# Deferring two of seven pair products, plain products in the experts, and block sums moved between VectorE and GpSimd

## The chip, the cores and the metric

One core of a Trainium2 chip runs the kernel. The metric is the device time of one execution in microseconds; the times are medians of several executions.

## The reference

Three layers follow one another: causal attention with a cumulative bias (2 batches, 8 heads, 576 rows, 64 columns), a mixture of 8 experts with a relu, weighted by gates P that come out of 8 rounds of row and column normalising, and one wide layer with a softplus.

```python
def _moe_ref(x, w_gate, w1, w2):
    ...
    for e in range(E):                    # E = 8, w1[e] 512 x 1024, w2[e] 1024 x 512
        h = np.maximum(x @ w1[e], 0.0)    # x: 1152 x 512
        ye = h @ w2[e]
        out += P[:, e:e + 1] * ye

def _moe2_ref(x, w_in, w_out):            # w_in 512 x 2048, w_out 2048 x 512
    h = x @ w_in
    g = np.maximum(h, 0.0) + np.log1p(np.exp(-np.abs(h)))
    return (g @ w_out).astype(np.float32)
```

## The kernel before

All matrix products keep float32 accuracy by splitting each operand into a high part (a copy rounded by ScalarE) and a low part (the word less its high part), and adding three products: high x high, high x low, low x high.

Both dense layers are cut into blocks of 512 hidden columns, x = 0 to 19: NX = 16 blocks of the experts and 4 of the wide layer (NH = 20). The 1152 rows are two batches g = 0, 1 of 576. Work runs as a pipeline of phases. The first phase of block x (here: its A phase) makes the up products of x for batch 1 and beside them the down products of x for batch 0; the second (B) makes the up products of x + 1 for batch 0 and the down products of x for batch 1. One tile of 128 rows, number 4 (NB), lies across both batches.

The up products are made by `Unit`, a seven-product scheme: p1 to p7 for each of two units a and b, 6 matmuls of 288 columns each. Unit results leave PSUM as words of h; `evict` (L452) does that, and `defer(k, ...)` puts it off by k + 1 calls of `flush`, of which each product and each down step makes one.

The down products exist in two forms. The plain one, `downs` (L555), takes a tile of 128 rows in 4 steps of three 512-column matmuls, and `total` adds the sum to acc. The other one, `pairs` (L389), makes a batch's 512 rows with seven products of blocks, each for r = 0 and 1: 14 steps of 6 matmuls with 256 columns. Its operands are four blocks a11, a12, a21, a22 of the words, and sums s1 to s4 of them, against the four blocks b of w2 and four sums t1 to t4. The products share PSUM halves: s2, a22, s1 and s4 accumulate one behind the other on the same half, and `add_to` (L376) adds the half to acc on VectorE after each of them, so that the next one on it must wait for that add. The blocks that use `pairs` are listed in SEVEN (L130): 14, 17, 18 and 19.

The preparation: `h_steps` (L322) makes sums (L334, GpSimd), high parts (L327, ScalarE) and low parts (L330, VectorE) of a batch's blocks, with m the part of the words that belongs to tile 4. `prep_t` (L248) makes the sums t (L256, GpSimd) and `t_part` their high (L243, ScalarE) and low parts (L245, VectorE); `prep_b` (L220) the parts of the blocks b (L226 ScalarE, L228 VectorE). `sums1`, `sums2` (GpSimd) and `split` (ScalarE, VectorE) prepare w1. One work tile xw holds s3, s2, t2 and t4 in turn; `hold` guards whose it is. In prep_t of a block that follows a block with pairs, two sums are written in place over raw b11 and b12.

The order is written out by hand in strings that `play` (L1289) reads: a1 to b7 are products, d is the next step of down work, and other tokens append a generator to one of three lists (back, side, bot). After each product and each d, `step` takes one step of the first generator of each list. Every engine runs its own instructions in this program order. In the A phase before, pair steps come in twos behind a product:

```python
A7_SEQ = "E0 a1 b1 a2 b2 =0 d d a6 d d b6 d d F0 a7 d d b7 =1 d d a5 d b5 d d a3 d b3 e1 a4 d b4"
B7_SEQ = ("E1 a1 b1 =2 a2 b2 d d d d a6 d d {11} b6 d d {3} F1 a7 d b7 d {2} a5 d b5 d {4} d a3 d {1} d b3 e0 d {22} a4 d b4 d {21}")
```

The last block has no products left in its second phase; that phase is called the tail.

Of the kernel before, what the change touches and what calls it, by code (L numbers as in the profile page):

```python
# [14 lines left out]
ALU = mybir.AluOpType  # L15
# [5 lines left out]
def attention_moe_ffn(ctx, tc, q, k, v, s, w_gate, w1, w2, w_in, w_out, out):  # L21
    nc = tc.nc
    P = 128
    B, S, H, D = v.shape
# [28 lines left out]
    def f(ap):  # L53
        return ap.bitcast(F32)
# [72 lines left out]
    w2_p = []  # L127
    w2_t = []
    sp_t = {}
    SEVEN = (NX - 2, NX + 1, NX + 2, NX + 3)  # L130

    def load(x, which, i):
        if x >= NH:
# [74 lines left out]
    def seven(x):  # L208
        return x in SEVEN

# [9 lines left out]
    def prep_b(x, n):  # L220

        if x >= NH:
            return
        raw = blocks(x)[n]
        hi, lo = (w2_block(n, z) for z in w2_t)
        nc.scalar.activation(out=hi, in_=raw, func=AF.Copy)  # L226
        yield
        nc.vector.tensor_tensor(out=lo, in0=raw, in1=f(hi), op=ALU.subtract)  # L228
        if n == "21":
            load(x + 1, 2, 1)  # L230
        ready.add((x, "b" + n))
        yield
# [3 lines left out]
    def hold(who, after):  # L236
        assert held[0] in after, (held, who)
        held[0] = who

    def t_part(x, n, src, part):  # L240
        h, l = (sp_t[z][:, n - 1] for z in ("th", "tl"))
        if part == "h":
            nc.scalar.activation(out=h, in_=src, func=AF.Copy)  # L243
        else:
            nc.vector.tensor_tensor(out=l, in0=src, in1=f(h), op=ALU.subtract)  # L245
            ready.add((x, f"t{n}"))

    def prep_t(x, n, kept=True):  # L248
# [73 lines left out]
    def h_steps(x, g, part):  # L322

        z = h_sets(g)

        def high(n):
            nc.scalar.activation(out=z[n][0], in_=z[n][2], func=AF.Copy)  # L327

        def low(n):
            nc.vector.tensor_tensor(out=z[n][1], in0=z[n][2], in1=f(z[n][0]), op=ALU.subtract)  # L330
            ready.add((x, g, n))

        def sum_(o, a, b, op):
            nc.gpsimd.tensor_tensor(out=z[o][2], in0=z[a][2], in1=z[b][2], op=op)  # L334

        if part == "e":
            hold((x, g), (None,))
            sum_("s3", "a11", "a21", ALU.subtract)
            high("a11")
            yield  # L340
            low("a11")
            yield
            last = (x - 1 + g, 1 - g)
            assert not seven(last[0]) or (*last, "done") in ready
            high("s3")
            yield
        elif part == "E":
            high("m")
            high("a22")
            yield  # L350
            low("s3")
            low("m")
            low("a22")
            sum_("s2", "a22", "s3", ALU.subtract)
            yield
            sum_("s1", "a21", "a22", ALU.add)
            yield
            high("a12")
            yield
            low("a12")  # L360
            high("s2")
            yield
            sum_("s4", "a12", "s2", ALU.subtract)
            high("s1")
            yield
            low("s2")
            low("s1")
            hold(None, ((x, g),))
            yield
        else:  # L370
            high("s4")
            yield
            low("s4")
            yield

    def add_to(x, t, cols, py, first, tile_col):  # L376
        a = acc[0][:, t, cols]
# [8 lines left out]
        if x == NH - 1 and (not first or (tile_col == (0, 1))):  # L386
            nc.sync.dma_start(out=out[t * P:(t + 1) * P, cols], in_=a)

    def pairs(x, g, middle=None):  # L389

        z = h_sets(g)
        py = []
        for r in range(2):
            nd[0] += 1
            py.append(ps.tile([P, DM], F32, tag=f"y{1 + nd[0] % 2}", name="py", bufs=1))
        d = (slice(0, HW), slice(HW, 2 * HW))

        def left(k, n, c, r):
            return z[n][k][:, c, r, :]

        def right(k, n, c):
            if n[0] == "t":
                return sp_t[("th", "tl")[k]][:, int(n[1]) - 1, c, :]
            return w2_block(n[1:], w2_t[k])[:, c, :]

        for a, b, bank, start, tile_, col, first in (
# [4 lines left out]
            if a == "s3" and middle is not None:  # L411
                yield from middle
            for r in range(2):
                assert (x, g, a) in ready and ((x, b) in ready or {(x, "w", 2 * (b[1] == "2") + c) for c in range(2)} <= ready), (x, g, a, b)
                o = py[r][:, d[bank]]
                for c in range(2):
                    ops = [(left(0, a, c, r), right(0, b, c)), (left(0, a, c, r), right(1, b, c)),
                           (left(1, a, c, r), right(0, b, c))]
                    for n, (u, v) in enumerate(ops):
                        nc.tensor.matmul(o, u, v, start=(start and c == 0 and n == 0), stop=(c == 1 and n == 2),  # L420
                                         skip_group_check=True)
                flush()
                if a == "s4" and r:
                    ready.add((x, g, "done"))
                add_to(x, rows_of(g) // P + 2 * r + tile_, d[col], o, first, (tile_, col))
                yield

# [58 lines left out]
    class Unit:  # L486
# [32 lines left out]
        def p2(self):  # L519
            b = self.bank("tr")  # L520
            self.product(b, A12, B21, True)
            flush()
            nc.vector.tensor_tensor(out=b, in0=b, in1=self.v1, op=ALU.add)  # L523
            evict(self.x, 5 if seven(self.x) else 0, b, self.p, self.h0)

        def p6(self):
            self.product(self.a, S2, T2, False)
# [8 lines left out]
        def p5(self):  # L536
            self.product(self.a, S1, T1, False)
            flush()
            u4 = self.copy("v")
            t = m_t[0].tile([P, HB], F32, tag="t2", name="t2", bufs=2)  # L540
            defer(0, lambda: nc.vector.tensor_tensor(out=t, in0=self.c, in1=u4, op=ALU.add))  # L541
            evict(self.x, 1, t, self.p + 2, self.h1)

        def p3(self):
            self.product(self.a, S4, B22, False)
# [57 lines left out]
    with tc.manual_schedule():  # L603
# [680 lines left out]
        def products(x, g):  # L1284

            u = dict(a=Unit(x, 0, g), b=Unit(x, 1, g))
            return {z: getattr(u[z[0]], "p" + z[1]) for z in ORDER.split()}

        def play(seq, todo, d=None):  # L1289


            for z in seq.split():
# [11 lines left out]
                if z[0] in "xy":  # L1304
                    bot.append(prep_b(x + 1, z[1:]) if z[0] == "x" else prep_t(x + 1, int(z[1]), seven(x)))
                    continue
                if z[0] in "eEF":
                    g = int(z[1])
                    if seven(x if g else x + (z[0] == "e")):
                        side.append(h_steps(x if g else x + (z[0] == "e"), g, z[0]))  # L1310
                    continue
                if z == "n":
                    flush()
# [7 lines left out]
        B_SEQ = ("d d =2 a1 d d b1 d a2 d b2 d a6 d b6 d a7 d b7 d a5 d b5 d d w0 a3 d d w2 b3 d d w1 a4 d d w3 b4")  # L1321
        A_TURN = "a1 b1 a2 b2 d d d d a6 =0 d b6 d a7 d b7 d =1 a5 d b5 d a3 d b3 d a4 d b4 d d d"
        TURN = ("t0 d d d d u0 d d d d d a1 d b1 d a2 d =2 b2 t1 d a6 d b6 d a7 d b7 d a5 d b5 d d u1 w0 a3 w2 b3 w1 a4 w3 b4")
        A7_SEQ = "E0 a1 b1 a2 b2 =0 d d a6 d b6 d d F0 a7 d d b7 =1 d d a5 d b5 d d a3 d b3 e1 a4 d b4"
        A7_LAST = "E0 a1 b1 a2 b2 d a6 d d b6 d d F0 a7 d d b7 d d a5 d b5 d a3 d b3 e1 a4 b4 d d"
        B7_SEQ = ("E1 a1 b1 =2 a2 b2 d d d d a6 d d {11} b6 d d {3} F1 a7 d b7 d {2} a5 d b5 d {4} d a3 d {1} d b3 e0 d {22} a4 d b4 d {21}")
        TO_SEVEN = B_SEQ.replace("b2", "b2 y3 y2 y4 y1").replace("b3", "b3 e0")
        B7 = {True: {"11": "x11 x12 y0", "3": "y3", "2": "y2", "4": "y4", "1": "y1", "22": "x22", "21": "x21"},
              False: {"11": "w0 w1", "3": "", "2": "", "4": "", "1": "", "22": "", "21": "w2 w3"}}
        A_GROUPS = [(0, 1), (2,), (3,)]  # L1330
        B_GROUPS = [(4,), (5,), (6,), (7, 8)]

        def then(*parts):
            for z in parts:
                yield from z
# [6 lines left out]
        for x in range(NH):  # L1342
# [6 lines left out]
            if x == NX - 2:  # L1349
                nc.scalar.preload_act_table_set("softplus")  # L1350
            if seven(x):
                play(A7_SEQ if x + 1 < NH else A7_LAST, products(x, 1), pairs(x, 0))
            else:
                play(A_SEQ if x != NX else A_TURN, products(x, 1), downs(x, A_GROUPS))
            if x == NX:
# [5 lines left out]
                own = open_blocks()  # L1361
            if seven(x):
                if x + 1 < NH:
                    seq = B7_SEQ
                    for k, z in B7[seven(x + 1)].items():
                        seq = seq.replace("{" + k + "}", z)
                    play(seq, products(x + 1, 0), then(downs(x, [(NB,)]), pairs(x, 1)))
                else:
                    play("E1 n n n n " + "d " * 8 + "F1 " + "d " * 10, {}, pairs(x, 1, downs(x, [(NB,)], "tr")))
                if not seven(x + 1):  # L1370
                    rest()
                    own.close()
                continue
# [70 lines left out]
```

## Time and profile before

| what | us |
|---|---|
| median of 3 runs | 1088.13 (1088.04 to 1088.27) |
| profiled execution | 1089.59 |
| its span, first to last instruction | 1087.80 |
| TensorE busy | 1056.2 |
| VectorE busy | 799.5 |
| ScalarE busy | 525.3 |
| GpSimd busy | 406.1 |

The profile shows one execution. Busy time of TensorE is that of matmuls in flight, which overlap, so its share is near 100% whenever it has work; starts of consecutive matmuls give the real pace. In rows of single instructions the columns are start, duration, engine, line and names, and in brackets the idle time in front and what ended it.

### The profile page before, as it was taken

How to read it: one execution, taken by the hardware profiler on the slowest of the kernel's cores; microseconds unless marked ns; L12 is line 12 of the kernel's file. 1: busy time of each engine (PE TensorE's matmuls, PEld its weight loads, DVE VectorE, ACT ScalarE, POOL GpSimd, SP SyncE). 2: the span in 40 equal slices, each digit the busy share in tenths (PEclk: the TensorE clock that was granted, in tenths of full speed). 3: DMA queues.
4: the chain of work that ended last, by engine and by line, in shares of the span. 5: the costliest groups of instructions: out<-in, count | busy, mean ns of one | idle time of the engine just before them, and what ended most of it. 6: DMA issues, size and time to landing. Idle time of an engine off the chain costs nothing.

```text
span 1087.8 us, 18435 instructions
## 1 busy us (share of the span) xinstructions
PE 1056.2 (97%) x6876; PEld 942.5 (87%) x6876; DVE 799.5 (73%) x1725; ACT 525.3 (48%) x1232; POOL 406.1 (37%) x449
## 2 busy tenths in 40 slices
PE   6999999999999999999999999999999999999987
PEld 4777888889888888988888898888899888898987
DVE  5576566667877878787887888775477487678876
ACT  6998544334443433434343343334454365555542
POOL 8885303053342414134241423423262233546321
PEclk9999999999999999999999999999999999999999
DMA  6221111122232222223222231311111011201002
GB/s 195 78 83 55 39 40 39 40 92 96 89 130 88 80 97 98 100 77 124 91 74 98 97 107 68 127 59 39 39 40 59 20 40 39 78 21 59 1 16 73
DMA packets 31538, 78.47 MB, mean 72 GB/s; under 512 B 5856, under 2 KB 13024, under 8 KB 31448
## 3 DMA queue, kind: packets, MB, share of 16 engines
q1 hardware_dynamic: 28704, 68.69, 18.9%
q0 software_dynamic: 2560, 8.39, 2.0%
q8 instruction: 54, 0.88, 0.3%
q14 instruction: 36, 0.29, 0.1%
q10 hardware_dynamic: 184, 0.20, 0.1%
HBM read 65.99 MB, written 10.75 MB: 71 GB/s over the span
## 4 chain that ended last, share of the span: by engine, by line
PE 82%; DVE 10%; ACT 3%; issue 2%; POOL 2%; DMA 0%; POOLq 0%; ACTq 0%; DVEq 0%
PE py L578 36%; PE ph L502 35%; PE py L420 5%; DVE hl L330 2%; PE sc L794 2%; POOL eb L857 1%; PE pv L901 1%; DVE sl L330 1%; PE tr L875 1%; DVE xl L1198 1%; DVE acc L381 1%; DVE xt L1229 1%; DVE ph L523 1%; PE sc L798 1%; DVE w1l L155 1%
## 5 line engine op out<-in xcount | busy, mean ns | idle before, releaser
L502 PE MATMUL ph<-xh,w1h 128*128 128x288 f32 x1120 | 331.7, 296 | 0.3 <-ACT v L510 0.3
L502 PE MATMUL ph<-xh,w1l 128*128 128x288 f32 x1120 | 330.8, 295 | 0.0
L502 PE MATMUL ph<-xl,w1h 128*128 128x288 f32 x1120 | 329.3, 294 | 0.0
L578 PE MATMUL py<-w2h,hh 128*128 128x512 f32 x588 | 233.5, 397 | 1.0 <-DVE acc L590 1.0
L578 PE MATMUL py<-w2l,hh 128*128 128x512 f32 x588 | 232.5, 395 | 0.2 <-POOL w2l L201 0.2
L578 PE MATMUL py<-w2h,hl 128*128 128x512 f32 x588 | 232.4, 395 | 0.0
L502 PEld LDWEIGHTS ph<-xh,w1h 128*128 128x128 f32 x1120 | 210.0, 188 | 18.4 <-ACT v L510 0.5
L502 PEld LDWEIGHTS ph<-xl,w1h 128*128 128x128 f32 x1120 | 210.4, 188 | 16.9
L502 PEld LDWEIGHTS ph<-xh,w1l 128*128 128x128 f32 x1120 | 210.3, 188 | 0.0
L510 ACT ACTIVATE v<-ph 128x288 f32<-128x288 f32 x160 | 64.0, 409 | 187.5 <-PE ph L502 184.8
L469 ACT ACTIVATE hh<-ph 128x288 fp32r<-128x288 f32 x180 | 73.7, 411 | 151.8 <-DVE ph L552 78.2
L578 PEld LDWEIGHTS py<-w2h,hl 128*128 128x128 f32 x588 | 110.5, 188 | 26.5
L201 POOL TENSOR_TENSOR w2l<-raw,w2h 128x512 fp32r<-128x512 f32 x36 | 51.3, 1427 | 215.9 <-ACT w2h L199 215.9
L596 DVE SCALAR_TENSOR_TENSOR acc<-py,gate,acc 128x512 f32<-128x512 f32 x118 | 88.0, 746 | 49.2 <-PE py L578 49.0
L1166 POOL TENSOR_TENSOR cm<-cm,ct 128x512 f32<-128x512 f32 x32 | 45.1, 1408 | 201.5 <-DVE ct L1164 201.5
L578 PEld LDWEIGHTS py<-w2h,hh 128*128 128x128 f32 x588 | 110.4, 188 | 10.5 <-DVE acc L590 1.2
L578 PEld LDWEIGHTS py<-w2l,hh 128*128 128x128 f32 x588 | 110.5, 188 | 10.0 <-POOL w2l L201 0.7
L155 DVE TENSOR_TENSOR w1l<-raw,w1h 128x512 fp32r<-128x512 f32 (+1 forms) x160 | 109.8, 686 | 11.3 <-ACT w1h L152 11.3
L476 DVE SCALAR_TENSOR_TENSOR hl<-ph,hh 128x288 fp32r<-128x288 f32 x180 | 81.2, 453 | 26.7 <-ACT hh L469 25.1
L152 ACT ACTIVATE w1h<-raw 128x512 fp32r<-128x512 f32 (+1 forms) x160 | 91.1, 571 | 0.0
L541 DVE TENSOR_TENSOR t<-ph,v 128x288 f32<-128x288 f32 x80 | 36.4, 455 | 54.5 <-ACT v L510 53.9
L510 ACT ACTIVATE u<-ph 128x288 f32<-128x288 f32 x80 | 32.7, 411 | 55.5 <-PE ph L502 53.4
(246 smaller groups left out, 1779.2 us busy)
## 6 DMA issues: line engine op xcount, KB each, us to landing
raw<-in_w SPq DMA_DIRECT2D x64, 512.0 KB
f<-in_w_in SPq DMA_DIRECT2D x16, 512.0 KB
f<-in_w_out SPq DMA_DIRECT2D x16, 512.0 KB
wd<-cm POOLq DMA_DIRECT2D x32, 256.0 KB, 3.1
raw<-wd SPq DMA_DIRECT2D x16, 512.0 KB
vv<-in_v SPq DMA_DIRECT2D x8, 256.0 KB
out<-acc SPq DMA_DIRECT2D x16, 128.0 KB
qk<-in_k SPq DMA_DIRECT2D x7, 288.0 KB
```

Source lines behind the costliest of these rows:

```text
L152: nc.scalar.activation(out=hi[:, o], in_=t[:, src], func=AF.Copy)
L155: nc.vector.tensor_tensor(out=lo[:, o], in0=t[:, src], in1=f(hi[:, o]), op=ALU.subtract)
L201: (nc.gpsimd if i else nc.vector).tensor_tensor(out=lo, in0=t[:, r], in1=f(hi), op=ALU.subtract)
L420: nc.tensor.matmul(o, u, v, start=(start and c == 0 and n == 0), stop=(c == 1 and n == 2), skip_group_check=True)
L469: nc.scalar.activation(out=hh, in_=z, func=AF.Relu)
L476: nc.vector.scalar_tensor_tensor(out=hl, in0=z, scalar=0.0, in1=f(hh), op0=ALU.max, op1=ALU.subtract)
L502: nc.tensor.matmul(o, u, v, start=(start and c == 0 and n == 0), stop=(c == 1 and n == 2), skip_group_check=True)
L510: nc.scalar.activation(out=t, in_=self.a, func=AF.Copy)
L541: defer(0, lambda: nc.vector.tensor_tensor(out=t, in0=self.c, in1=u4, op=ALU.add))
L578: nc.tensor.matmul(py[t], u, v, start=(k == 0 and n == 0), stop=(k == NF - 1 and n == 2))
L596: nc.vector.scalar_tensor_tensor(out=a, in0=py, scalar=gate_t[0][:, t, e:e + 1], in1=a, op0=ALU.mult, op1=ALU.add)
L1166: nc.gpsimd.tensor_tensor(out=m, in0=m, in1=f(t), op=ALU.add)
```

## The change

SEVEN loses block 14, so that no block of the experts uses pair products. In h_steps the sums go from GpSimd to VectorE; in prep_b and t_part the low parts go from VectorE to GpSimd. The last two of the seven pair products (s4 and a12, four steps) of a batch are made in the phase behind, in front of its own down work, one behind each of the first four products; each of the other ten pair steps then stands behind one product. The steps of h_steps begin with their phase (part E, 13 steps; F is s4's high and low part) instead of in the phase before (part e). The words of p2 and p5 are deferred further. The parts of b22 and b21 are made in the A phase (X22, X21) instead of at the end of the B phase before.

```diff
-    SEVEN = (NX - 2, NX + 1, NX + 2, NX + 3)
+    SEVEN = (NX + 1, NX + 2, NX + 3)
...   prep_b, t_part
-        nc.vector.tensor_tensor(out=lo, in0=raw, in1=f(hi), op=ALU.subtract)
+        nc.gpsimd.tensor_tensor(out=lo, in0=raw, in1=f(hi), op=ALU.subtract)
...
-            nc.vector.tensor_tensor(out=l, in0=src, in1=f(h), op=ALU.subtract)
+            nc.gpsimd.tensor_tensor(out=l, in0=src, in1=f(h), op=ALU.subtract)
...   h_steps
-            nc.gpsimd.tensor_tensor(out=z[o][2], in0=z[a][2], in1=z[b][2], op=op)
...
+            nc.vector.tensor_tensor(out=z[o][2], in0=z[a][2], in1=z[b][2], op=op)
+        if part == "F":
+            assert (x, g, "s3 done") in ready
             high("s4")
             yield
             low("s4")
             yield
+            return
+        hold((x, g), (None,))
+        sum_("s3", "a11", "a21", ALU.subtract)
+        high("m")
+        yield
+        high("a11")
+        low("m")
+        yield
+        high("a22")
+        low("a11")
+        yield
+        low("a22")
+        yield
+        last = (x - 1 + g, 1 - g)
+        assert not seven(last[0]) or (*last, "s4 done") in ready
+        high("s3")
+        yield
+        low("s3")
+        yield
+        sum_("s2", "a22", "s3", ALU.subtract)
+        yield
+        high("a12")
+        yield
+        sum_("s1", "a21", "a22", ALU.add)
+        yield
+        high("s2")
+        yield
+        low("s2")
+        yield
+        low("a12")
+        high("s1")
+        yield
+        sum_("s4", "a12", "s2", ALU.subtract)
+        low("s1")
+        hold(None, ((x, g),))
+        yield
...   Unit.p2, Unit.p5
-            evict(self.x, 5 if seven(self.x) else 0, b, self.p, self.h0)
+            evict(self.x, 8 if seven(self.x) else 0, b, self.p, self.h0)
...
-            evict(self.x, 1, t, self.p + 2, self.h1)
+            evict(self.x, 4 if seven(self.x) else 1, t, self.p + 2, self.h1)
...   the order
+        A7_SEQ = ("E0 a1 ~ b1 ~ {22} a2 ~ b2 ~ {21} =0 a6 d b6 d a7 d b7 d F0 =1 a5 d b5 d a3 d b3 d a4 d b4 d")
+        B7_SEQ = ("E1 a1 d b1 d a2 d b2 d =2 a6 d d b6 d d {12} a7 d d {11} b7 d d {3} F1 a5 d b5 d {2} a3 d b3 d {4} a4 d b4 d {1}")
+        B7 = {True: {"12": "x12", "11": "x11 y0", "3": "y3", "2": "y2", "4": "y4", "1": "y1"},
...
+        A7 = {True: {"~": "d", "{22}": "X22", "{21}": "X21"}, False: {"~": "", "{22}": "", "{21}": ""}}
+        LAST = "E1 d d D d D d D D d d d d F1 " + "d " * 10
...
+                d = then(d if seven(x - 1) else (), pairs(x, 0))
+                play(seq, products(x, 1), d)
...
+                    d = then(d, downs(x, [(NB,)]), pairs(x, 1))
...
+                    play(LAST, {"D": lambda: next(middle)}, then(d, pairs(x, 1)))
```

## Rows read from the trace of the kernel before

**Rows 1.** The page's first part: busy time and share by engine.
```profile
PE 1056.2 (97%) x6876; PEld 942.5 (87%) x6876; DVE 799.5 (73%) x1725; ACT 525.3 (48%) x1232; POOL 406.1 (37%) x449
```

**Rows 2.** Windows: blocks 13, 14, 17, 18, block 19's first phase, tail.
```profile
core 0: us, PE busy (x) PEld busy (x) DVE busy (x) ACT busy (x) POOL busy (x), PEclk, DMA share, GB/s
742.77:790.25 47.48, 47.48 (x279) 42.56 (x277) 25.05 (x47) 18.84 (x45) 15.26 (x15) 1.00 0.13 45
790.25:839.85 49.60, 45.85 (x352) 44.70 (x351) 39.68 (x75) 25.63 (x57) 18.60 (x16) 1.00 0.16 54
942.30:993.03 50.73, 46.34 (x350) 44.61 (x349) 42.09 (x72) 27.93 (x62) 25.83 (x21) 1.00 0.12 42
993.03:1043.29 50.26, 46.31 (x350) 44.59 (x349) 42.15 (x74) 27.20 (x61) 24.40 (x20) 1.00 0.07 22
1043.29:1066.32 23.03, 21.52 (x170) 21.11 (x168) 16.03 (x32) 10.51 (x25) 5.53 (x4) 1.00 0.10 35
1066.32:1087.80 21.48, 15.45 (x98) 14.10 (x96) 13.86 (x24) 3.47 (x7) 3.98 (x3) 0.90 0.22 74
```

**Rows 3.** Timeline of TensorE: first matmuls of consecutive steps.
```profile
992.33 0.28 PE L420 MATMUL py<-w2h,hh 128*128 128x256 f32 x1
...
993.03 0.29 PE L502 MATMUL ph<-xh,w1h 128*128 128x288 f32 x1
...
993.83 0.29 PE L502 MATMUL ph<-xh,w1h 128*128 128x288 f32 x1
```

**Rows 4.** Waits of TensorE: total us, times, longest.
```profile
PE py L420 <- DVE acc L381: 8.3, 10, 2.2
```

**Rows 5.** Timeline of TensorE: gaps in block 14, block 18 and the tail.
```profile
823.24 0.38 PE L420 MATMUL py<-w2h,hh 128*128 128x256 f32 x1 [1.69 <-DVE acc L596]
...
1024.86 0.38 PE L420 MATMUL py<-w2h,hh 128*128 128x256 f32 x1 [1.33 <-DVE acc L593]
...
1075.16 0.36 PE L420 MATMUL py<-th,sh 128*128 128x256 f32 x1 [2.23 <-DVE acc L381]
```

**Rows 6.** Timeline of GpSimd, then VectorE, in the second phase of block 18.
```profile
1031.49 1.29 POOL L256 TENSOR_TENSOR raw<-raw,raw 128x512 f32<-128x512 f32 x1 [1.28 <-issue]
1032.72 1.75 POOL L256 TENSOR_TENSOR xw<-raw,raw 128x512 f32<-128x512 f32 x1
...
1031.61 1.71 DVE L330 TENSOR_TENSOR sl<-hw,sh 128x512 fp32r<-128x512 f32 x1
...
1033.58 1.44 DVE L245 TENSOR_TENSOR tl<-raw,th 128x512 fp32r<-128x512 f32 x1
```

**Rows 7.** Lines by themselves: duration in ns, min/median/max, first and last start.
```profile
L228 DVE TENSOR_TENSOR w2l<-raw,w2h x8: 675/678/692, 977.9 to 1047.5; 128x512 fp32r<-128x512 f32 x8
...
L381 DVE TENSOR_TENSOR acc<-py,acc x84: 407/416/427, 948.0 to 1084.4; 128x256 f32<-128x256 f32 x84
...
L201 POOL TENSOR_TENSOR w2l<-raw,w2h x36: 1283/1304/1772, 111.9 to 943.7; 128x512 fp32r<-128x512 f32 x36
...
L168 POOL TENSOR_TENSOR raw<-raw x4: 730/738/743, 954.7 to 1007.5; 128x256 f32<-128x256 f32 x4
...
L327 ACT ACTIVATE hh<-hw x40: 407/632/642, 786.9 to 1071.1; 128x512 fp32r<-128x512 f32 x32, 128x256 fp32r<-128x256 f32 x8
```

**Rows 8.** Timeline of VectorE, second phase of block 18: instructions right behind one another.
```profile
1036.20 0.46 DVE L541 TENSOR_TENSOR t<-ph,v 128x288 f32<-128x288 f32 x1 [0.48 <-ACT v L510]
1036.57 0.75 DVE L381 TENSOR_TENSOR acc<-py,acc 128x256 f32<-128x256 f32 x2
...
1039.99 0.69 DVE L245 TENSOR_TENSOR tl<-xw,th 128x512 fp32r<-128x512 f32 x1 [0.57 <-ACT th L243]
1040.60 0.42 DVE L381 TENSOR_TENSOR acc<-py,acc 128x256 f32<-128x256 f32 x1
```

**Rows 9.** Timeline of TensorE in the tail, behind its longest gap.
```profile
1076.97 0.42 PE L420 MATMUL py<-tl,hh 128*128 128x256 f32 x1
...
1079.75 0.41 PE L420 MATMUL py<-th,hl 128*128 128x256 f32 x1
```

More of the change, by code (lines that the diff above doesn't have):

```diff
@@ L333, in sum_ @@
         def sum_(o, a, b, op):
-            nc.gpsimd.tensor_tensor(out=z[o][2], in0=z[a][2], in1=z[b][2], op=op)
[L336 to L370, printed above, removed]
+            nc.vector.tensor_tensor(out=z[o][2], in0=z[a][2], in1=z[b][2], op=op)
+        if part == "F":
+            assert (x, g, "s3 done") in ready
             high("s4")
@@ L387, in add_to, with pairs @@
             nc.sync.dma_start(out=out[t * P:(t + 1) * P, cols], in_=a)
-    def pairs(x, g, middle=None):
+    def pairs(x, g):
         z = h_sets(g)
@@ L410, in pairs @@
                 ("a12", "b21", 1, True, 0, 0, False)):
-            if a == "s3" and middle is not None:
-                yield from middle
             for r in range(2):
@@ L422, in pairs @@
                 flush()
-                if a == "s4" and r:
-                    ready.add((x, g, "done"))
+                if r:
+                    ready.add((x, g, a + " done"))
                 add_to(x, rows_of(g) // P + 2 * r + tile_, d[col], o, first, (tile_, col))
@@ L1306, in play @@
                     continue
[L1307 to L1310, printed above, removed]
+                if z[0] in "EF":
+                    side.append(h_steps(x, int(z[1]), z[0]))
+                    continue
+                if z[0] == "X":
+                    bot.append(prep_b(x, z[1:]))
                     continue
@@ L1323, in attention_moe_ffn @@
         TURN = ("t0 d d d d u0 d d d d d a1 d b1 d a2 d =2 b2 t1 d a6 d b6 d a7 d b7 d a5 d b5 d d u1 w0 a3 w2 b3 w1 a4 w3 b4")
[L1324 to L1329, printed above, removed]
+        A7_SEQ = ("E0 a1 ~ b1 ~ {22} a2 ~ b2 ~ {21} =0 a6 d b6 d a7 d b7 d F0 =1 a5 d b5 d a3 d b3 d a4 d b4 d")
+        B7_SEQ = ("E1 a1 d b1 d a2 d b2 d =2 a6 d d b6 d d {12} a7 d d {11} b7 d d {3} F1 a5 d b5 d {2} a3 d b3 d {4} a4 d b4 d {1}")
+        TO_SEVEN = B_SEQ.replace("b2", "b2 y3 y2 y4 y1")
+        B7 = {True: {"12": "x12", "11": "x11 y0", "3": "y3", "2": "y2", "4": "y4", "1": "y1"},
+              False: {"12": "", "11": "w0 w1", "3": "", "2": "", "4": "", "1": "d d d d w2 w3"}}
+        A7 = {True: {"~": "d", "{22}": "X22", "{21}": "X21"}, False: {"~": "", "{22}": "", "{21}": ""}}
+        LAST = "E1 d d D d D d D D d d d d F1 " + "d " * 10
         A_GROUPS = [(0, 1), (2,), (3,)]
@@ L1351, in attention_moe_ffn @@
             if seven(x):
-                play(A7_SEQ if x + 1 < NH else A7_LAST, products(x, 1), pairs(x, 0))
+                seq = A7_SEQ
+                for k, z in A7[seven(x - 1)].items():
+                    seq = seq.replace(k, z)
+                d = then(d if seven(x - 1) else (), pairs(x, 0))
+                play(seq, products(x, 1), d)
             else:
@@ L1366, in attention_moe_ffn @@
                         seq = seq.replace("{" + k + "}", z)
-                    play(seq, products(x + 1, 0), then(downs(x, [(NB,)]), pairs(x, 1)))
+                    play(seq, products(x + 1, 0), d)
                 else:
-                    play("E1 n n n n " + "d " * 8 + "F1 " + "d " * 10, {}, pairs(x, 1, downs(x, [(NB,)], "tr")))
+                    middle = downs(x, [(NB,)], "tr")
+                    play(LAST, {"D": lambda: next(middle)}, then(d, pairs(x, 1)))
                 if not seven(x + 1):
```

## Prediction

> **What bounds the kernel now.** I read the page's first part first: TensorE is busy for 97% of the span [rows 1], so a change pays only by taking matmuls away or by closing gaps between them. Then the busy times by block. A plain block takes 47.48 us and TensorE is busy in all of it; block 14, the first with pair products, takes 49.60; blocks 17 and 18 take 50.73 and 50.26; block 19 has a first phase of 23.03 and a tail of 21.48, and in the tail the granted clock is 0.90 [rows 2].
>
> What these would take without gaps follows from starts of matmuls [rows 3]: a pair product for one r takes 0.70 us (992.33 to 993.03), a product of a Unit 0.80 (993.03 to 993.83); a step of a plain tile takes 0.70 too, since block 13 holds 28 products and 36 such steps (47.48 - 22.4, over 36) [rows 2]. A seven-product block has 28 products, 28 pair steps and 4 plain steps: 22.4 + 19.6 + 2.8 = 44.8 us. So the gaps are 5.93 us in block 17, 5.46 in block 18, 23.03 - 14 x 0.80 - 14 x 0.70 = 2.03 in block 19's first phase. The tail holds 18 steps, 12.6 us; its matmuls end near 1084.16, which is 17.84 after its start: 5.24 lost. Together 18.66 us.
>
> What ends these gaps: mostly an accumulation on VectorE (L381, 8.3 us in 10 waits) [rows 4], that is, TensorE wants the PSUM half which VectorE has not yet added to acc. Block 14 shows the same, there for the last plain block's add, L596; block 18 for the plain tile's add, L593; the longest, 2.23 us, is in the tail [rows 5]. After it matmuls start 0.21 us apart, 14 of them from 1076.97 to 1079.75 [rows 9], instead of 0.12 (six in 0.70), which is the lower of the two clock levels, 1.2 GHz; that alone is some 1.4 of the tail's 5.24.
>
> VectorE isn't slow at these adds; it is late. Of two operands in SBUF, its subtraction takes 0.68 us undisturbed [rows 7] and the next begins 0.60 after it (1039.99 to 1040.60) [rows 8]. But the one at 1031.61 took 1.71 and the one at 1033.58 took 1.44, and GpSimd worked from 1031.49 to 1032.78 and, itself stretched to 1.75, from 1032.72 to 1034.47 [rows 6]. Each ends 0.55 us after GpSimd's instruction: the two engines exclude each other when both read two SBUF operands. Adds out of PSUM take one SBUF operand only; two behind one another take 0.75, 0.33 more than one [rows 7, 8].
>
> **Part one: block 14 becomes plain.** It loses 28 pair steps and one plain tile and gets nine plain tiles: 36 steps of 0.70 against 32, +2.8 us of matmuls. It also loses its gaps. The row to take is that of block 13, which does exactly this work: 47.48 instead of 49.60, -2.12 us. No preparation of block sums is left there that could make a new gap.
>
> **Part two: the swap of engines.** Per block, 8 block sums of activations go from GpSimd (1.29) to VectorE (0.60), and 8 low parts of the weights go from VectorE to GpSimd. VectorE, in starts behind one another [rows 8]: 28 pair adds x 0.33, a plain one of 0.60, 12 additions of products x 0.37, 28 operations of 512 columns on SBUF x 0.60, 4 of 256 x 0.33: 32.4 us before and after. GpSimd [rows 7]: 8 + 4 instructions of 1.30 and 8 of 0.73, 21.4 us, before and after. The loads do not change; the order does. Before, each step from a block sum to its high part waited for a 1.29 us GpSimd instruction with VectorE's low parts behind it. Now the sum is made in VectorE's own queue.
>
> A rule speaks against this part. First the row: VectorE was busy 42.15 of 50.26 us in block 18 [rows 2], 9.8 more than its 32.4 of work, so it waited for nearly half of GpSimd's time. The Trainium skill (Perfetto Trace Analysis, "Optimizing Scalar/DVE Operations") says that the two engines share an SBUF read port, so moving work between them might not help. By it, part two would be worth nothing. The rows here agree about the port [rows 6], but the swap moves work between moments too, which the rule doesn't speak of.
>
> **Part three: the order.** The last two pair products (4 steps) go into the next phase, and every pair step now stands behind a product. The distance between two uses of one PSUM half grows from 0.70 x 2 + 0.80 = 2.2 us to 3.0; an operand's low part is issued 5 to 8 steps ahead of its use. I followed VectorE's queue through each phase with the durations of rows 7 and 8 and mutual exclusion as in rows 6.
>
> Block 17's first phase: low a11 is done 3.5 to 4.1 us in, its use is at 4.0: 0.5 us left (bounds 0 to 2). The second phases of 17 and 18: the sum, high, low chain ends at 11.0, the plain tile's add at 11.6, and it is wanted at 11.9; a little is lost later where ScalarE waits for GpSimd's sums before high t3, with the copy queued behind it that b3 needs: 0.5 each (0 to 1.5).
>
> The first phases of 18 and 19 get a new wait. GpSimd's list in the second half of the phase before is now serial: low b12, low b11, two sums in raw, then low t3, sum t2, low t2, sum t4, low t4. b11 is free only when its pair product ends, 12.8 us into the 23.8 us phase. From there [rows 7]: 0.65 (ScalarE) + 1.3 + 2 x 1.3 + 0.65 + 1.3 + 1.3 + 0.65 + 1.3 + 1.3 + 0.65 + 1.3, 13.0 in all, so 25.8, plus 0.4 to 2 for exclusion (each of VectorE's three subtractions there can take a turn of 0.6): low t4 ends 2.4 to 4.0 us into the next phase; I take 3.0, nearer to the lower end, since VectorE has little on SBUF in that stretch. The first thing VectorE has to do there, sum s3, writes xw, which low t4 reads. So VectorE's whole queue stands behind it, four deferred accumulations among them. After it come low t1, low b22, four w1 sums and low b21 on GpSimd, alternating with VectorE. By my list the accumulation of a12, r 0 is then done at 8.5 us; its PSUM tile is wanted at 6.8 by the next a11: 1.8 lost. That of r 1 is done at 10.8 to 12.1 against 10.2: 0.6 to 1.9 more, plus some 0.3 for the refilled pipeline. 3.3 us in block 18 (bounds 0, if low t4 comes before the phase; 6, if it comes 1.5 later and loses every turn at the port), 3.0 in block 19, where the w1 sums are missing (0 to 5).
>
> The tail has 22 steps instead of 18, but 4 fewer stand before it, and no GpSimd work. By the same list: 0.75 us for m's low part, 0.45 for s2's, 0.75 for an add, 0.3 refill: 2.2 (1 to 5.24, as now), none long enough to be like the 2.23 us gap that the clock fell after.
>
> The load of the next w2 half moves from the end of a phase to some 11 us into the next, behind GpSimd's low b21. It is wanted 25 us later; the queue behind it on SyncE holds only w1 loads for the phase after. Nothing.
>
> Sum of gaps: 0.5 + 0.5 + 3.3 + 0.5 + 3.0 + 2.2 = 10.0 instead of 18.66: -8.7 us. With block 14: -10.8. The profiled execution took 1089.59 us, with a span of 1087.80; it lies 1.46 above the median of the runs, so 1078.8 for it and 1077.3 for the median.
>
> **Rivals.**
> Clean: sum s3 does not wait, since GpSimd gets through in time, and all first phases run free. For it: the chain without exclusion ends only 2.0 us into the phase. Then gaps are some 2.5 to 4 us, 1088.13 - 2.12 - 15.4 = 1070.6.
> Late: GpSimd loses each turn at the port; 9 instructions at 1.75 [rows 6] instead of 1.30 bring low t4 to about 6 us. Then 18 and 19 lose 6 and 5, the second phases 1.5 each, the tail 3: 0.5 in 17's first: gaps of 17.5, 1084.8.
> Unchanged: VectorE waits for the same share of GpSimd's time as now, its queue is as late at the new places as at the old, and the gaps stay 18.66 in sum; only block 14 pays: 1088.13 - 2.12 = 1086.0. For it: neither load falls. Against: the longer distance at the PSUM halves. This is where the Trainium skill's sentence (Perfetto Trace Analysis, as above) would lead.
> Slower: the port becomes the bound. If VectorE waits for all of GpSimd's time, a block takes 32.4 + 21.4 = 53.8 us, with a share f of it 32.4 + 21.4 f. Now f is 9.8 / 21.4 = 0.46; from 0.85 a block is longer than today's 50.5. At f = 1, blocks 17 and 18 cost 3.3 more each and 19's first phase some 2, with block 14 -2.1 and a tail as now: 1094.6. For it: GpSimd now has work in the same stretch as VectorE's chain. Against: over two fifths of VectorE's work (14.3 of 32.4) is from PSUM and runs beside GpSimd.
>
> **How the numbers follow.** Forecast 0.50 (own range 1073 to 1081), clean 0.22, late 0.13, unchanged 0.07, slower 0.08. All of forecast, clean and late are faster by over 0.2% (below 1085.95), unchanged counts as same; 0.2% is about what a measurement of this kernel can tell from no change. So faster 0.85, same 0.07, slower 0.08. The range leaves out the best end of clean, and of the top the slower case: 1069.5 to 1086.0.
>
> **What would show it.** Block 14 at 47.5 us right behind block 13. In blocks 18 and 19, TensorE's gaps at the first two a11 steps, ended by L381's adds, and behind them VectorE's sum s3 waiting for GpSimd's low t4; no gap over 0.5 us at s3 or s2. Subtractions on GpSimd near 1.30 us. In the tail a clock of 1.00. I am wrong if a gap opens at an operand's low part, if block 17's first phase has gaps too, or if VectorE's busy time per block grows beyond 42 us.

## Result: 1.0% faster, and where it came from

The changed kernel takes 1077.85 us (median of 4 runs, 1077.27 to 1078.27) against 1088.09 us before; the ratio is 0.9905 with a 95% interval of 0.9888 to 0.9923. The forecast was 1077.3. Its profiled execution took 1078.24 us with a span of 1076.50. Part of the spread of the runs lies ahead of the change: the two runs with a mean granted clock of 0.998 take 1078.24 and 1078.27, those with 0.999 and 1.000 take 1077.27 and 1077.46; what the traces show of that is in the last section, and rows from block 13 on are free of it.

The first part of its page, to stand beside [rows 1]:

```profile
PE 1056.5 (98%) x6804; PEld 938.7 (87%) x6804; DVE 777.3 (72%) x1705; ACT 514.5 (48%) x1212; POOL 382.6 (36%) x433
```

The busy times by block, to stand beside [rows 2] (columns as there). The lines are block 13, block 14, then both phases of 17, both of 18, the first of 19, and the tail:

```profile
core 0: us, PE busy (x) PEld busy (x) DVE busy (x) ACT busy (x) POOL busy (x), PEclk, DMA share, GB/s
742.24:789.72 47.48, 47.48 (x278) 42.56 (x277) 24.24 (x49) 17.47 (x41) 8.42 (x10) 1.00 0.13 45
789.72:837.20 47.48, 47.48 (x278) 42.56 (x277) 24.26 (x49) 18.75 (x42) 8.42 (x10) 1.00 0.14 45
939.85:958.75 18.90, 18.75 (x146) 18.28 (x145) 17.49 (x32) 11.45 (x28) 9.44 (x9) 1.00 0.16 56
958.75:983.40 24.65, 24.27 (x182) 23.35 (x181) 20.38 (x38) 13.22 (x30) 10.46 (x8) 1.00 0.13 44
983.40:1006.66 23.26, 22.21 (x171) 21.18 (x169) 19.69 (x35) 13.37 (x31) 14.22 (x13) 1.00 0.14 46
1006.66:1031.32 24.66, 24.28 (x183) 23.35 (x181) 20.34 (x38) 13.20 (x30) 10.48 (x8) 1.00 0.00 1
1031.32:1054.57 23.25, 21.72 (x171) 21.10 (x169) 17.38 (x32) 11.29 (x27) 5.97 (x5) 1.00 0.04 13
1054.57:1076.50 21.93, 17.24 (x122) 15.44 (x120) 15.04 (x32) 4.92 (x9) 0.00 (x0) 0.99 0.28 96
```

Without gaps these six phases take 18.2, 23.8, 21.0, 23.8, 21.0 and, up to the last matmul, 15.4 us (0.80 per product, 0.70 per step). What is over is each phase's gaps. The tail's last matmul's slot ends at 1072.83, 18.26 after its start.

| phase | gaps foreseen, us | measured |
|---|---|---|
| 17, first | 0.5 | 0.70 |
| 17, second | 0.5 | 0.85 |
| 18, first | 3.3 | 2.26 |
| 18, second | 0.5 | 0.86 |
| 19, first | 3.0 | 2.25 |
| tail | 2.2 | 2.86 |
| sum (before: 18.66) | 10.0 | 9.78 |

The spans of the two profiled executions differ by 11.30 us: 2.12 in block 14 (49.60 to 47.48, the length of block 13 to the hundredth), 8.88 in blocks 17 to 19 (18.66 to 9.78), 0.53 ahead of block 13, where the change touches nothing (over the kernels of this study block 13 starts between 741.1 and 742.8 us), and -0.2 in blocks 15 and 16. The profiled execution of before lay 1.50 above its median of 1088.09 and that of after 0.39, which is why the medians differ by 10.24.

The new wait, in the first phase of block 18. The chain that ended last (start, duration, what) leaves TensorE there and comes back 14 us later:

```profile
983.57 0.81 PE ph L503 x6
...
984.38 1.30 POOL tl L245
...
985.70 0.69 DVE xw L334
986.39 0.33 DVE acc L384
986.73 1.71 DVE hl L330 x2
...
990.51 0.32 DVE acc L384
...
998.37 0.95 PE py L421 x6
```

Low t4 on GpSimd begins at 984.38 and ends 2.3 us into the phase; VectorE's sum s3 (L334, writing xw) starts 0.02 us later, and all accumulations stand behind it. The waits of VectorE say the same (total us, times, longest):

```profile
DVE xw L334 <- POOL tl L245: 3.3, 2, 1.7
```

TensorE's gaps in blocks 18 and 19, from an idle time of 0.2 us up, are these (timeline of TensorE; idle time and its end in brackets; a matmul starts some 0.15 us later against its slot than its bracket says, since matmuls overlap). The first three and the last two stand behind the new wait:

```profile
990.98 0.36 PE L421 MATMUL py<-w2h,hh 128*128 128x256 f32 x1 [0.40 <-DVE acc L384]
992.97 0.38 PE L421 MATMUL py<-w2h,hh 128*128 128x256 f32 x1 [0.26 <-DVE acc L384]
998.37 0.36 PE L421 MATMUL py<-th,sh 128*128 128x256 f32 x1 [0.37 <-DVE acc L384]
1020.83 0.35 PE L421 MATMUL py<-th,sh 128*128 128x256 f32 x1 [0.38 <-DVE acc L384]
1038.89 0.36 PE L421 MATMUL py<-w2h,hh 128*128 128x256 f32 x1 [0.39 <-DVE acc L384]
1041.76 0.39 PE L421 MATMUL py<-w2h,hh 128*128 128x256 f32 x1 [1.14 <-DVE acc L384]
```

The two first are the two a11 steps of block 18's pair products, the two last those of block 19. The line at 1020.83 lies in block 18's second phase and has another cause, told below.

### The profile page after: what moved, and what is told of

Same layout as the page of the kernel before. It is cut to its first block, busy times and chain, and to the rows that moved or that the text cites. A ratio compares the mean times of both kernels' runs of the same rounds, so it can differ in the third digit from the quotient of the medians.

```text
span 1076.5 us, 18205 instructions
## 1 busy us (share of the span) xinstructions
PE 1056.5 (98%) x6804; PEld 938.7 (87%) x6804; DVE 777.3 (72%) x1705; ACT 514.5 (48%) x1212; POOL 382.6 (36%) x433
## 4 chain that ended last, share of the span: by engine, by line
PE 88%; DVE 6%; POOL 2%; ACT 2%; issue 1%; DMA 1%; SPq 0%; POOLq 0%; ACTq 0%; DVEq 0%
PE py L579 39%; PE ph L503 39%; PE py L421 4%; PE sc L795 1%; PE pv L902 1%; POOL eb L858 1%; DVE hl L330 1%; PE tr L876 1%; DVE xl L1199 1%; DVE acc L384 1%; DVE xt L1230 1%; PE sc L799 0%; ACT eb L845 0%; PE tr L870 0%; DVE xw L334 0%
## 5 line engine op out<-in xcount | busy, mean ns | idle before, releaser
L579 PE MATMUL py<-w2h,hh 128*128 128x512 f32 x620 | 246.2, 397 | 1.0 <-DVE acc L591 1.0
L579 PE MATMUL py<-w2l,hh 128*128 128x512 f32 x620 | 245.1, 395 | 0.2 <-POOL w2l L201 0.2
L579 PE MATMUL py<-w2h,hl 128*128 128x512 f32 x620 | 245.1, 395 | 0.0
L470 ACT ACTIVATE hh<-ph 128x288 fp32r<-128x288 f32 x192 | 78.5, 411 | 159.9 <-DVE ph L553 80.8
L579 PEld LDWEIGHTS py<-w2h,hl 128*128 128x128 f32 x620 | 116.5, 188 | 28.0
L597 DVE SCALAR_TENSOR_TENSOR acc<-py,gate,acc 128x512 f32<-128x512 f32 x126 | 93.9, 746 | 56.2 <-PE py L579 56.1
L579 PEld LDWEIGHTS py<-w2h,hh 128*128 128x128 f32 x620 | 116.4, 188 | 10.8 <-DVE acc L591 1.2
L579 PEld LDWEIGHTS py<-w2l,hh 128*128 128x128 f32 x620 | 116.6, 188 | 10.3 <-POOL w2l L201 0.7
L477 DVE SCALAR_TENSOR_TENSOR hl<-ph,hh 128x288 fp32r<-128x288 f32 x192 | 86.5, 452 | 31.2 <-ACT hh L470 29.5
```

Of the source, the lines that this page charges most:

```text
L470: nc.scalar.activation(out=hh, in_=z, func=AF.Relu)
L477: nc.vector.scalar_tensor_tensor(out=hl, in0=z, scalar=0.0, in1=f(hh), op0=ALU.max, op1=ALU.subtract)
L579: nc.tensor.matmul(py[t], u, v, start=(k == 0 and n == 0), stop=(k == NF - 1 and n == 2))
L597: nc.vector.scalar_tensor_tensor(out=a, in0=py, scalar=gate_t[0][:, t, e:e + 1], in1=a, op0=ALU.mult, op1=ALU.add)
```

## Experiments

All are timed against the kernel before, whose medians were 1088.05 us in the first set of four and 1088.22 in the second.

### Each part alone

**Block 14 plain, nothing else** (plain14):

```diff
-    SEVEN = (NX - 2, NX + 1, NX + 2, NX + 3)
+    SEVEN = (NX + 1, NX + 2, NX + 3)
```

> The kernel before with one edit: block 14 leaves SEVEN. Theory (the parts add up): block 14 takes 47.48 us like block 13, the gaps of blocks 17 to 19 stay at some 18.7 us in sum, so 1086.0 us. Rival (block 14's pairs also delay what follows, or hide something): blocks 15 to 17 move too, and the time is under 1085 or over 1087.5.

Measured: 1087.15 us, ratio 0.9985 (0.9975 to 0.9994). Block 14 by itself:

```profile
788.68:836.16 47.48, 47.48 (x278) 42.56 (x277) 24.25 (x49) 18.77 (x42) 8.44 (x10) 1.00 0.14 45
```

The block is 2.12 us shorter, as worked out from block 13's row, and blocks 17 and 18 are as before (50.76 and 50.26). In this execution the tail took 18.93 us to its last matmul at a granted clock of 0.82, against 17.84 at 0.90 before, so the gaps of blocks 17 to 19 sum to 19.78 here. The median moved by 0.9 only. The ten runs went from 1084.93 to 1088.54, by and large the faster the higher their mean granted clock (1.000 down to 0.995). At a mean clock of 0.998 three runs took 1085.82 to 1086.05, and those of the kernel before 1087.78 to 1088.16: 2.0 us, as the block's row says.

**The swap of engines in the old order, with block 14 plain** (swap_only): plain14 and

```diff
-        nc.vector.tensor_tensor(out=lo, in0=raw, in1=f(hi), op=ALU.subtract)
+        nc.gpsimd.tensor_tensor(out=lo, in0=raw, in1=f(hi), op=ALU.subtract)
...
-            nc.vector.tensor_tensor(out=l, in0=src, in1=f(h), op=ALU.subtract)
+            nc.gpsimd.tensor_tensor(out=l, in0=src, in1=f(h), op=ALU.subtract)
...
-            nc.gpsimd.tensor_tensor(out=z[o][2], in0=z[a][2], in1=z[b][2], op=op)
+            nc.vector.tensor_tensor(out=z[o][2], in0=z[a][2], in1=z[b][2], op=op)
```

> As plain14, and the engines swapped (block sums on VectorE, weights' low parts on GpSimd) in the old order. Theory (the order brings the gain, and a late low t4 on GpSimd holds VectorE's sum s3): in the old order the sum s3 follows low t4 within one phase, so VectorE's queue stands behind it for 3 us or more, and the gaps do not shrink: 1085 to 1092 us. Rival 1 (the swap itself is what helps, since a block sum no longer costs a GpSimd hop): gaps fall to 10 to 13, 1078 to 1081. Rival 2 (moving work between two engines on one port is worth nothing): 1086.

Measured: 1091.41 us, ratio 1.0030 (1.0019 to 1.0040), 4.3 us more than plain14. Blocks 17 and 18:

```profile
938.77:993.50 54.73, 49.03 (x350) 47.55 (x349) 39.86 (x75) 27.03 (x61) 22.23 (x19) 0.94 0.12 39
993.50:1045.31 51.81, 45.88 (x350) 44.53 (x349) 37.82 (x72) 25.80 (x58) 22.83 (x20) 1.00 0.06 22
```

The time lies where the theory put it, but not for its reason. The wait of sum s3 on low t is 3.5 us in 3 waits over all blocks, the longest 1.8. Two others are larger. First, most pair steps come in twos (ten of 14; in the kernel's string one d stands behind a6, not two), and the sums now stand in VectorE's queue between a product and the add that the next step wants (timeline of VectorE, then TensorE):

```profile
945.23 0.85 DVE L334 TENSOR_TENSOR hw<-hw 128x512 f32<-128x512 f32 x1
946.00 0.45 DVE L523 TENSOR_TENSOR ph<-ph,v 128x288 f32<-128x288 f32 x1
946.37 0.41 DVE L381 TENSOR_TENSOR acc<-py,acc 128x256 f32<-128x256 f32 x1
...
946.83 0.38 PE L420 MATMUL py<-th,sh 128*128 128x256 f32 x1 [2.52 <-DVE acc L381]
```

Second, GpSimd has low b in front of the sums in raw, so high t3 comes late on ScalarE, and the copy behind it too, on which VectorE's next addition and the adds behind that depend (timelines of ScalarE, VectorE, TensorE):

```profile
982.66 0.63 ACT L243 ACTIVATE th<-raw 128x512 fp32r<-128x512 f32 x1 [5.12 <-POOL raw L256]
983.20 0.39 ACT L510 ACTIVATE v<-ph 128x288 f32<-128x288 f32 x1
...
983.62 0.46 DVE L541 TENSOR_TENSOR t<-ph,v 128x288 f32<-128x288 f32 x1 [3.17 <-ACT v L510]
...
984.47 0.38 PE L420 MATMUL py<-th,hh 128*128 128x256 f32 x1 [2.03 <-DVE acc L381]
```

Block 17 also shows a granted clock of 0.94; the last section comes back to that. The gaps of blocks 17 to 19 sum to 24.28 us, 4.5 more than plain14's, and slow steps at the lower clock are part of both sums.

**The new order on the old engines** (order_only): the changed kernel with those three operations as before (the same three lines, reversed).

> The changed kernel with its three moved operations back on their old engines: new order alone. Theory: the order carries most of the gain; sums on GpSimd add a hop of 0.7 us each but operands have 5 us to spare, and no wait of VectorE on low t4; 1076.5 to 1080 us. Rival 1 (the swap matters as much): 1081 to 1085. Rival 2 (nothing from the swap): 1077.9 as the changed kernel.

Measured: 1078.45 us, ratio 0.9909 (0.9893 to 0.9926). Its gaps sum to 10.36 us. They lie elsewhere; the two phases of 17, both of 18, and the first of 19:

```profile
938.91:958.77 19.86, 19.05 (x147) 18.41 (x145) 16.30 (x29) 11.29 (x27) 16.05 (x14) 1.00 0.17 54
958.77:984.77 26.00, 24.53 (x182) 23.41 (x181) 21.42 (x39) 13.41 (x31) 9.78 (x7) 1.00 0.12 42
984.77:1006.75 21.98, 21.51 (x171) 21.07 (x169) 19.75 (x35) 12.99 (x30) 15.44 (x13) 1.00 0.15 49
1006.75:1033.08 26.33, 24.56 (x183) 23.43 (x181) 21.72 (x39) 13.44 (x31) 9.77 (x7) 1.00 0.00 1
1033.08:1054.08 21.00, 21.00 (x171) 21.00 (x169) 16.19 (x32) 11.01 (x27) 7.60 (x5) 1.00 0.04 14
```

Block 19's first phase has no gap at all (21.00), and 18's has 0.98. The wait on xw is still there and as long, but it is now GpSimd's: its sum s3 waits for VectorE's low t4, and VectorE's adds don't stand behind it in a queue (timeline of GpSimd, blocks 18 and 19):

```profile
986.08 1.30 POOL L334 TENSOR_TENSOR xw<-hw 128x512 f32<-128x512 f32 x1 [1.71 <-DVE tl L245]
1034.38 1.30 POOL L334 TENSOR_TENSOR xw<-hw 128x512 f32<-128x512 f32 x1 [1.72 <-DVE tl L245]
```

But the second phases take 26.00 and 26.33, gaps of 2.2 and 2.5 where the changed kernel has 0.85, since all eight low parts are VectorE's again in the phase that has most work, and 17's first phase loses 1.66, 0.33 of it idle time at an operand's low part (949.69), which the expectation had 5 us to spare. So the order carries the gain, 8.7 of it over plain14, and the swap shifts gaps from second phases into first ones; 0.6 us in its favour, in the medians as in the sums of gaps. The runs overlap (1077.88 to 1079.15 against 1077.27 to 1078.27); taken by mean granted clock, two and two, they don't, so the 0.6 is likely real, but not established by so few.

**Block 14 with pairs, in the changed kernel** (pairs14):

```diff
-    SEVEN = (NX + 1, NX + 2, NX + 3)
+    SEVEN = (NX - 2, NX + 1, NX + 2, NX + 3)
```

> The changed kernel with block 14 back in SEVEN. Theory: the matmuls of pairs take 44.8 us against 47.48 for plain ones, and in the new order the gaps of a first block are some 1.6 us, with the gate's factor in the adds a little more: block 14 takes 46.3 to 47.0, the time is 0.5 to 1.2 below the changed kernel's: 1077.0. Rival (pairs in the experts lose as they did before, 4.8 us of gaps): block 14 takes 49.6, 1080.0.

Measured: 1076.01 us, ratio 0.9887 (0.9872 to 0.9902). Block 14:

```profile
788.60:834.90 46.30, 45.92 (x351) 44.61 (x350) 42.14 (x85) 25.33 (x58) 9.44 (x9) 1.00 0.17 58
```

46.30 us, 1.18 below a plain block and 3.30 below the same products in the old order. The pairs were never the loss in the experts; their order was. The medians differ by 1.8, more than the 0.5 to 1.2 expected; the row accounts for 1.2. Of the rest most is the clock: the three runs at 1.000 took 1075.90 to 1076.11, 1.2 to 1.6 below the changed kernel's two at 0.999 and 1.000.

### The wait on xw

**Low parts of t on VectorE** (tlow_dve): the changed kernel and

```diff
     # t_part
-            nc.gpsimd.tensor_tensor(out=l, in0=src, in1=f(h), op=ALU.subtract)
+            nc.vector.tensor_tensor(out=l, in0=src, in1=f(h), op=ALU.subtract)
```

> The changed kernel with the low parts of t1 to t4 back on VectorE (sums of activations on VectorE, low parts of the blocks b on GpSimd). Theory (VectorE's queue stands behind sum s3, which waits for GpSimd's low t4 on xw): low t4 is done before the phase ends, sum s3 does not wait, the first phases of 18 and 19 lose under 1 us each instead of 2.26 and 2.25, and the time falls by 2 to 3 us against the changed kernel, to some 1075.3. Rival 1 (those gaps come from taking turns at the port, whatever xw does): they stay near 2 us and the time within 0.7 of the changed kernel's. Rival 2 (2.4 us more of work per block on VectorE make it late elsewhere): 1079 or more.

Measured: 1075.15 us, ratio 0.9878 (0.9863 to 0.9893). The first phases of 18 and 19, with 18's second between them:

```profile
982.69:1004.89 22.20, 21.25 (x171) 21.04 (x170) 20.29 (x37) 13.05 (x31) 10.71 (x10) 1.00 0.15 48
1004.89:1029.88 24.99, 24.55 (x182) 23.39 (x181) 22.24 (x40) 13.55 (x31) 8.54 (x6) 1.00 0.00 1
1029.88:1051.04 21.16, 21.16 (x171) 21.04 (x169) 17.24 (x34) 10.92 (x27) 2.86 (x2) 1.00 0.04 14
```

19's first phase went from 2.25 us of gaps to 0.16, 18's from 2.26 to 1.20, the second phases up from 0.86 to 1.19: VectorE's 1.9 us more of busy time in such a phase (22.24 against 20.34) cost 0.3. The gaps sum to 7.32, 2.5 less than in the changed kernel. At the start of block 18's first phase, sum s3 now follows VectorE's own low t4, 1.3 us into the phase instead of 2.3:

```profile
983.23 0.68 DVE L245 TENSOR_TENSOR tl<-xw,th 128x512 fp32r<-128x512 f32 x1
983.95 0.69 DVE L334 TENSOR_TENSOR xw<-hw 128x512 f32<-128x512 f32 x1
```

Low t4 is done 1.2 us into the phase, not before it as expected, and the expectation for block 18, under 1 us, was missed by 0.2.

**Only the two that are read from xw** (xwlow_dve): as before, but

```diff
+            (nc.vector if n in (2, 4) else nc.gpsimd).tensor_tensor(out=l, in0=src, in1=f(h), op=ALU.subtract)
```

> The changed kernel with the low parts of t2 and t4 alone, the two that are read from xw, back on VectorE. Theory: the same as for all four, as sum s3 waits for the reader of xw only; low t1 on GpSimd still takes a turn in the next phase: 1075.3 to 1076.3. Rival 1 (turns at the port): within 0.7 of the changed kernel's.

Measured: 1075.31 us, ratio 0.9879 (0.9865 to 0.9894). The first phases of 18 and 19 lose 1.60 and 0.80, the second ones 0.88 and 0.86 as in the changed kernel; the gaps sum to 7.71 against 7.32 for all four. So of the 2.1 us that block 19's first phase won, 1.45 go with the two that are read from xw, and the other 0.64 with low t1 and t3. In block 18 the split is 0.66 and 0.40. The larger part isn't the wait alone: sum s3 begins 1.25 us into block 19's first phase instead of 2.28, and with the queues shifted against each other sum s2 no longer meets GpSimd's low b21 there (0.67 us instead of 1.74). Rival 1, turns between the two engines, holds for the smaller part: GpSimd makes low t1 beside VectorE's low a11, which takes 1.53 us here and 0.68 in tlow_dve.

**All eight low parts on VectorE** (lows_dve): tlow_dve and prep_b's low part on VectorE too; the sums stay there.

> The changed kernel with all eight low parts of the weights back on VectorE: the block sums stay there too, so VectorE has 37.2 us of work per block and GpSimd 11. Theory (VectorE's lateness is its work plus nearly half of GpSimd's time): 37.2 + 0.46 x 11 = 42.3 us, as before, no wait on xw either: 1075 to 1077.5. Rival (VectorE needs the relief): its busy time per block passes 44 us and gaps open at the accumulations: 1079 or more.

Measured: 1076.76 us, ratio 0.9890 (0.9874 to 0.9907). Block 18:

```profile
984.09:1031.70 47.61, 46.11 (x350) 44.54 (x349) 42.88 (x81) 26.53 (x61) 12.41 (x12) 1.00 0.07 23
```

VectorE is busy for 42.88 us, against 42.3 worked out as its work plus nearly half of GpSimd's time. Its gaps, 8.15 in sum, are 0.8 above tlow_dve's, most of them in the second phases (1.66 each); the medians are 1.6 apart, but three of the four runs here have a mean clock of 0.998 and one of tlow_dve's. Work shifted from GpSimd to VectorE costs little here, but it costs.

**Both remedies** (tlow_p14): tlow_dve with block 14 back in SEVEN.

> Low parts of t1 to t4 back on VectorE and block 14 back in SEVEN. Theory (the two effects lie in different blocks and add): block 14 in 46.3 us, 18 and 19 without the wait on xw, 1.2 to 1.9 below the first kernel of this set: some 1073.7. Rival: block 14's gaps grow with VectorE's load and the gain of 1.2 is lost.

Measured: 1074.07 us, ratio 0.9867 (0.9852 to 0.9882), the fastest kernel here. Block 14 takes 46.30 (789.72 to 836.02), as in pairs14, and the gaps of 17 to 19 sum to 7.28, as in tlow_dve: the two add. Its median is 1.1 us below tlow_dve's, where 1.2 to 1.9 were expected; its two runs at a mean clock of 0.999 and 1.000 took 1073.57 and 1073.59, 1.6 below the three of tlow_dve at 1.000.

## Why the prediction was right, step by step

Block 14: the term of -2.12, taken from block 13's row, came out to the hundredth, in the changed kernel and alone.

The swap: "the loads do not change; the order does" held. VectorE was busy for 19.69 + 20.34 = 40.03 us in block 18, 7.6 over its 32.4 of work, against 9.8 before, so it waited for a third of GpSimd's time instead of nearly half. The Trainium skill's sentence that moving work between the two engines might not help (Perfetto Trace Analysis, "Optimizing Scalar/DVE Operations") is what the runs show of this swap by itself: 0.6 us, not established, in the new order, and a loss of 4.3 in the old one, part of it at the lower clock. The rival made of it was wrong all the same, since the order was worth 8.7. The prediction didn't part these two; its sum came out right without it.

The order: in blocks 17 and 18 and in block 19's first phase no gap is ended by a late high or low part of an operand; the tail has 0.54 us at tile 4's low m, foreseen at 0.75, and under 0.2 at s2's low part, foreseen at 0.45. The rest are adds.

The new wait: the place and the chain were right, some sizes not. Low t4 ended 26.9 us after the second phase of 17 had begun (958.75 to 985.67), as taken (23.8 + 3.0); but that phase was 24.65 us long, so this is 2.3 us into the next one, not 3.0 and just below the bound of 2.4. The accumulation of a12 for r 0 was done at 7.4 (990.42 and 0.41 after it) instead of 8.5, hence 2.26 and 2.25 us of gaps rather than 3.3 and 3.0. Block 19's was expected to be smaller than 18's, without the w1 sums; it was the same, because there GpSimd's low b21 came right in front of VectorE's sum s2, which took 1.74 us, and the add for r 1 stood behind it: the 1.14 us at 1041.76 (timelines of GpSimd and VectorE).

```profile
1039.54 1.28 POOL L228 TENSOR_TENSOR w2l<-raw,w2h 128x512 fp32r<-128x512 f32 x1 [2.05 <-ACT w2h L226]
...
1039.63 1.74 DVE L334 TENSOR_TENSOR xw<-hw,xw 128x512 f32<-128x512 f32 x1
```

The wait alone would not have made the accumulation of a12 late. Between sum s3 and it stand the low parts of m, a11 and a22, which GpSimd's low t1 and low b22 stretched (1.79 us for the first two and 1.44 for the third, where tlow_dve has some 1.0 and 0.68). Without these 1.5 us it would by estimate have been done at 5.9 us into the phase, ahead of the 7.0 at which its tile was wanted (990.98, less the 0.55 by which that step came late). The prediction's list had both terms, the wait and the turns, and both were needed.

Which add a pair step waits for was put wrongly. I let it be the last one on the same PSUM half, and counted s2, a22, s1 and s4 to one half. In `pairs` a11, s2, s1 and s4 write one half and s3, a22 and a12 the other. But s3 began at 1020.83 behind an add of a11, and s2 at 998.37 behind the add of s3 for its r (timeline of VectorE), which is on the other half; the add before it on its own half, a11's, had ended at 994.60:

```profile
997.80 0.42 DVE L384 TENSOR_TENSOR acc<-py,acc 128x256 f32<-128x256 f32 x1
```

So the wait is for the last add on the whole tile; whether the chip asks for that or the way the program sets its semaphores, no run here shows. The 2.2 and 3.0 us, which I gave as distances between two uses of a half, are those between two uses of a tile. By halves, s2 follows a11 only two products later. The two slips cancelled in the sum, which is luck, but the gaps at s2 and s3 did not stand on my list.

Block 17 and the second phases: 0.70, 0.85 and 0.86 against 0.5 each, and not where they were foreseen. In 17's first phase the gaps stand at the two a22 steps (953.04 and 954.94), ended by adds, and not at low a11; the prediction's last paragraph names gaps there as a sign against it, though its own list has 0.5. In the second phases there is none in front of b3. The largest there is the gap at 1020.83 (in block 17 at 972.91): two steps of a11 follow one another there, and VectorE had w1's low part, held up by GpSimd's low b, in front of a11's add.

The tail: 2.86 against 2.2, and no fall of the clock, as foreseen (0.99 over a stretch that includes the end, against 0.90 before). The longest idle time in it is 0.56 us.

That the sum came within 0.3 us of gaps has luck in it: the first phases of 18 and 19 were 1.8 too high, the other four terms 1.6 too low.

Left open: what the remaining 1.2 us in block 18's first phase need (low b22, b21 and the w1 sums on GpSimd are still in it, but lows_dve without the first two still has 1.16), the 2.9 of the tail, which all variants of the new order share, and which part of the new order (the deferred products, the steps one by one, the moved preparation, the later words) brings how much of its gain.

## What to carry to other kernels

When one engine's in-order queue releases another's buffers, count what stands ahead of the release, not how busy the engine is: the new order as a whole, in which a PSUM tile is used again after 3.0 instead of 2.2 us, brought 8.7 us in the medians with the loads unchanged. Before moving an operation to a slower engine, look at who reuses its input: one work tile shared by two chains put VectorE's whole queue behind a single late reader, and moving two subtractions back took 2.1 us of gaps away, while as long a wait on the same tile in GpSimd's queue left block 19's first phase without a gap. And a form that loses in one order (pairs in block 14, 49.60 against 47.48) may win in another (46.30), so drop it only after the order is settled.

## What the runs showed of the hardware

That VectorE and GpSimd exclude each other when both read two SBUF operands was seen before; after, GpSimd's subtractions show both faces of it, 1.29 us alone and 1.75 or so behind VectorE (lines by themselves, ns as min/median/max):

```profile
L228 POOL TENSOR_TENSOR w2l<-raw,w2h x8: 1277/1288/1730, 970.6 to 1039.5; 128x512 fp32r<-128x512 f32 x8
L245 POOL TENSOR_TENSOR tl<-raw,th x4: 1293/1526/1765, 977.7 to 1033.7; 128x512 fp32r<-128x512 f32 x4
```

Not expected: in the swapped kernel in the old order the lower clock level came back in the midst of dense work. Behind the idle time of 2.52 us that ends at 946.83, the granted clock was 0.54, and behind one of 2.03 us, which ends at 984.47, it was 0.70; behind one of 2.04 us, ended by an add at 1037.80, it stayed at 1.00 (windows; columns as in the table by block):

```profile
948.50:952.00 3.50, 3.50 (x18) 3.27 (x17) 2.12 (x6) 2.27 (x5) 0.00 (x0) 0.54 0.02 5
984.40:988.00 3.60, 3.53 (x21) 3.54 (x22) 1.37 (x5) 1.72 (x5) 2.78 (x4) 0.70 0.00 0
1034.00:1040.00 6.00, 3.96 (x33) 3.76 (x32) 1.91 (x5) 2.41 (x6) 4.44 (x5) 1.00 0.00 0
```

So the price of a gap can be more than its length (the step from 948.55 to 949.99 took 1.44 us instead of 0.70), and the length of the gap alone doesn't tell whether that price is paid.

In four traces the clock also fell early, behind shorter idle times. In the attention, all ten traces have an idle time of TensorE of some 1.0 us that ends between 16.2 and 16.5 us. In four of them (before, after, lows_dve, tlow_p14) another one, of 0.59 to 1.05 us, ends 2.2 us ahead of that, and from 18 to 21 us the granted clock is 0.50 to 0.59; in the other six that one is at most 0.23 us, and the clock stays at 1.00. Block 13 begins at 742.2 to 742.8 us in the four, at 741.1 to 741.5 in the six. This is likely most of the 1 us by which runs of one kernel in the new order differ, and no part of the change.
